# Attention and gated feed-forward on one core: six of seven score tiles transposed by DMA from pair 12, and row sums, v scaling and instruction order rewritten

## The chip, the cores and the metric

The kernel runs on one core of one Trainium2 chip. The metric is the device time of one execution in microseconds (us); lower is better. The core has five engines with a queue each: TensorE (PE; its weight loads are shown apart as PEld), VectorE (DVE), ScalarE (ACT), GpSimd (POOL) and SyncE (SP). Here SP issues every DMA. Each queue runs its instructions strictly in the order in which the program puts them.

## The reference

Eight batches of twelve heads, 448 rows of 64 numbers each. First q and k are normalised by row, then softmax attention, then a feed-forward block with a convolution over three neighbours and a sigmoid gate (q, k, v, the weights and the output are float32; the weights of the second part reach the kernel as float64).

```python
def rmsnorm(x, g):
    rms = np.sqrt(np.mean(x * x, axis=-1, keepdims=True) + 1e-06)
    return x / rms * g
q_n, k_n = (rmsnorm(q, g_q), rmsnorm(k, g_k))
scores = 1.0 / np.sqrt(q.shape[-1]) * np.matmul(q_n, k_n.transpose(0, 1, 3, 2))
attn = np.exp(scores - np.max(scores, axis=-1, keepdims=True))
attn = attn / (np.sum(attn, axis=-1, keepdims=True) + 1e-9)
x = np.matmul(attn, v)                 # then heads side by side: [8, 448, 768]
h = np.maximum(x @ w_in, 0.0)          # [8, 448, 1024]
conv_out = sum(conv_w[k] * hp[:, k:k + S, :] for k in range(3))   # hp: h padded by a row
out = (h * (1 / (1 + np.exp(-conv_out)))) @ w_out                 # [8, 448, 768]
```

## The kernel before

**Pairs.** The 96 heads are worked on two at a time: 48 pairs, n = 0 to 47, six to a batch. A pair's 896 query rows are cut into seven tiles of 128, the slots (`SLOTS`, line 510). One slot's scores are a 128x448 tile.

**Attention of a pair.** `load_k`, `load_q` and `v_load` bring 224 KB each. `square` and `square_sum` (line 349) make the sums of squares, `rsqrt` inverts the root by Newton steps, `apply_rms` scales, `qk_transpose` turns q and k on TensorE, and `qk_hi`/`qk_lo` write each as a high and a low float16 half. `scores` multiplies with three float16 products per slot (high by high, low by high, high by low). `soft_max` (DVE), then `soft_exp` (ACT), which also writes the row sums into `rsum`.

**Two ways to turn a slot.** The product with v needs the exponentials e transposed. In the first way `p_transpose` (line 582) does it on TensorE with four float32 transposes, and `p_evac` (line 589) copies the result from PSUM to `PT`. In the second way `p_hi` and `p_lo` (lines 560, 568) split e into two float16 halves in a buffer `ph`, and `p_turn` (line 575) turns both halves in one DMA transpose from `ph` to `PT`. `nd(n)` (line 516) says how many slots of a pair go the second way: none for n below `n1` = 8, then 4.

**The product with v.** `pv` (line 652) first multiplies the columns that came through TensorE in float32 (eight products of 64 rows; 448 columns each where no slot goes by DMA, 192 with four slots by DMA), and then those that came by DMA as 24 float16 products (256 columns with four slots). For it `v_scaled` (line 631) multiplies v in place by a power of two, `v_hi` (line 637) casts that to float16 and `v_lo` (line 640) subtracts to get the low half.

**The row sums.** `sum_step` (line 596) adds 1e-9 and inverts the 128x7 tile `rsum` on DVE, `sum_transpose` (line 604) turns it on TensorE, `sum_evac` copies it to `rT`, `sum_store` writes it to DRAM (`rd`), and two `sum_load` read it back over all partitions (`rB`). `x_scale` (line 674) multiplies the product by it.

**The feed-forward.** After six pairs a batch's eight `in_part` groups (line 736; 18 products of 448 columns each) run, with relu, convolution, tanh and gate on ACT, DVE and POOL, and then the `out_part` groups (line 798; 24 products of 384 columns each). They are spread between the pairs of the next batches. Until about 140 us the kernel also converts the weights on DVE.

**What sets the order.** Every step has a planned due time (`at`), what it needs (`needs`, line 915), and a cost on each engine that may run it (`options`, line 1167). A planner in the kernel simulates the engines with these, picks one ready step after another, and so fixes both the engine of each step and the order of every queue before the program is made. `PH` (line 20) holds its numbers, `BUFS` (line 104) the count of buffers of each kind: `ph` 3, `PT` 2, `e` 3, and two PSUM buffers `t` for everything that TensorE transposes. `LAT` (line 1297) says how long after a step's end another engine may use it.

```
521:        if ("PT", n) not in rings.setdefault("PT", Ring(BUFS["PT"])).d:
575:    def p_turn(n, j):
577:        nc.sync.dma_start_transpose(
1046:            yield "pv", n - BUFS["PT"], pvs(n - BUFS["PT"])[-1]
1298:        "PE": dict(PE=0.0, DVE=0.2, ACT=0.2, POOL=0.2, SP=0.2, DMA=0.2),
1299:        "DVE": dict(PE=0.06, DVE=0.13, ACT=0.13, POOL=0.16, DMA=0.17),
```

## Time and profile before

| What | Value |
|---|---|
| Median of 3 runs | 979.03 us (978.38 to 981.58) |
| The profiled execution | 978.28 us |
| its span, first to last instruction | 976.5 us |
| PE busy | 893.8 us, 92% |
| DVE busy | 777.3 us, 80% |
| ACT busy | 680.4 us, 70% |
| POOL busy | 660.1 us, 68% |
| DMA: share of the 16 engines' span, hardware queue | 52.1% |

The profile is of one execution. Busy time is the time in which an engine ran at least one instruction. The span is 1.8 us shorter than that execution's own time. A window table gives busy time for stretches of the span and the clock that TensorE was granted, where 1.00 is its upper level, 2.4 GHz, and 0.50 the lower, 1.2 GHz.

### The profile page before, as it was taken

How to read it: one execution, taken by the hardware profiler on the slowest of the kernel's cores; microseconds unless marked ns; L12 is line 12 of the kernel's file. 1: busy time of each engine (PE TensorE's matmuls, PEld its weight loads, DVE VectorE, ACT ScalarE, POOL GpSimd, SP SyncE). 2: the span in 40 equal slices, each digit the busy share in tenths (PEclk: the TensorE clock that was granted, in tenths of full speed). 3: DMA queues.
4: the chain of work that ended last, by engine and by line, in shares of the span. 5: the costliest groups of instructions: out<-in, count | busy, mean ns of one | idle time of the engine just before them, and what ended most of it. 6: DMA issues, size and time to landing. Idle time of an engine off the chain costs nothing.

```text
span 976.5 us, 18886 instructions
## 1 busy us (share of the span) xinstructions
PE 893.8 (92%) x6590; PEld 522.6 (54%) x6590; DVE 777.3 (80%) x1349; ACT 680.4 (70%) x1564; POOL 660.1 (68%) x723
## 2 busy tenths in 40 slices
PE   1777688978999799999999999999999999999988
PEld 0344344545656366655665566556665665556545
DVE  6999979899689967699789977898889966992540
ACT  3678667776666777679688776788788776785331
POOL 2489868886687758498688767587778864772120
PEclk9788669998999999999999999999999999999999
DMA  9945423343773677555765667446684565244001
GB/s 215 247 105 148 126 57 76 64 101 71 155 160 75 107 125 149 116 110 103 153 133 122 125 133 148 102 92 139 144 163 92 109 148 100 51 94 107 17 16 50
DMA packets 259759, 111.02 MB, mean 114 GB/s; under 512 B 220928, under 2 KB 256080, under 8 KB 259664
## 3 DMA queue, kind: packets, MB, share of 16 engines
q1 hardware_dynamic: 259664, 109.82, 52.1%
q8 instruction: 52, 0.85, 0.3%
q14 instruction: 43, 0.35, 0.1%
HBM read 56.65 MB, written 11.18 MB: 69 GB/s over the span
## 4 chain that ended last, share of the span: by engine, by line
PE 49%; DVE 12%; POOL 6%; issue 3%; ACT 3%; DMA 1%; SPq 0%; POOLq 0%; ACTq 0%; DVEq 0%
POOL ph L89 1%; POOL gring L89 1%; POOL sq L89 1%; DMA PT<-ph 1%; DVE st L351 1%; DVE ph L89 1%; POOL x L89 1%; POOL st L386 1%; DVE c_(1_4_3520 L763 0%; POOL st L375 0%; DVE carry L788 0%; PE m_('o'_7_0_0_12066 L812 0%; PE m_('o'_5_3_0_10563 L812 0%; PE m_('o'_3_3_0_7531 L812 0%; PE m_('o'_1_3_0_4495 L812 0%
## 5 line engine op out<-in xcount | busy, mean ns | idle before, releaser
L742 PEld LDWEIGHTS <-wi 128*128 128x128 f16 x1152 | 108.7, 98 | 99.8 <-issue 16.6
L812 PEld LDWEIGHTS <-gring 128*128 128x128 f16 (+1 forms) x1056 | 101.3, 100 | 66.4 <-issue 16.9
L89 POOL TENSOR_TENSOR sq<-qkf,st 112x512 f32<-112x512 f32 x80 | 96.0, 1214 | 2.8 <-ACT wi L254 1.0
L89 POOL TENSOR_TENSOR x<-rB,x 128x448 f16<-128x448 f32 x48 | 57.2, 1191 | 49.3 <-ACT x L77 39.5
L633 POOL TENSOR_SCALAR v<-v,vsc 112x512 f32<-112x512 f32 x42 | 72.0, 1718 | 17.8 <-DVE vsc L186 16.1
L543 PEld LDWEIGHTS <-qT 64*128 64x128 f16 x864 | 32.5, 96 | 71.1 <-issue 55.5
L351 DVE TENSOR_REDUCE st<-sq 112x16 f32<-112x1024 f32 x48 | 58.0, 1209 | 3.2 <-ACT sq L345 2.4
L669 PEld LDWEIGHTS <-vp 112*64 112x64 f16 x960 | 51.1, 110 | 9.7 <-issue 7.8
L441 POOL COPY qz<-qT 64x128 f16<-64x128 f16 x90 | 37.4, 416 | 25.8 <-DVE qT L432 23.1
L89 POOL TENSOR_TENSOR vp<-v,vp 112x512 f16<-112x512 f32 x38 | 46.3, 1219 | 8.9 <-ACT vp L77 6.6
L345 ACT ACTIVATE sq<-qkf 112x1024 f32<-112x1024 f32 x33 | 34.9, 1059 | 4.5 <-DMA qkf<-in_q_dram 4.5
L89 POOL TENSOR_TENSOR sq<-qkf 112x1024 f32<-112x1024 f32 x15 | 30.1, 2005 | 4.5 <-PE t_('qk'_7_0_1418 L412 2.3
L471 DVE TENSOR_REDUCE vacc<-v 112x1 f32<-112x512 f32 x48 | 32.2, 671 | 0.3
L77 ACT CAST vp<-v 112x512 f16<-112x512 f32 x36 | 22.2, 618 | 11.4 <-PE m_('v'_18_4614 L669 3.4
L600 DVE TENSOR_SCALAR rsum<-rsum 128x7 f32<-128x7 f32 x48 | 20.8, 432 | 8.2 <-ACT e_(29_6_7231 L555 1.5
L812 PEld LDWEIGHTS <-carry 128*64 128x64 f16 x192 | 20.2, 114 | 10.8 <-issue 4.1
L375 POOL TENSOR_SCALAR st<-st 112x32 f32<-112x32 f32 (+1 forms) x53 | 19.1, 360 | 10.0 <-DVE st L388 4.2
L386 POOL TENSOR_TENSOR st<-st 112x32 f32<-112x32 f32 (+1 forms) x25 | 10.1, 406 | 22.5 <-DVE st L381 19.4
L812 PEld LDWEIGHTS <-wi 128*128 128x128 f16 (+1 forms) x192 | 19.6, 102 | 9.3 <-ACT wi L77 0.5
L788 DVE COPY carry<-gring 128x128 f16<-128x128 f16 x32 | 19.2, 599 | 5.8 <-POOL gring L89 5.8
L543 PEld LDWEIGHTS <-qz 128*128 128x128 f16 x144 | 14.1, 100 | 16.5 <-issue 6.4
L89 DVE TENSOR_TENSOR sq<-qkf,st 112x512 f32<-112x512 f32 x16 | 22.7, 1424 | 0.0
(3733 smaller groups left out, 3134.2 us busy)
## 6 DMA issues: line engine op xcount, KB each, us to landing
qkf<-in_k_dram SPq DMA_DIRECT2D x48, 224.0 KB
qkf<-in_q_dram SPq DMA_DIRECT2D x48, 224.0 KB
v<-in_v_dram SPq DMA_DIRECT2D x48, 224.0 KB
rB<-rd SPq DMA_DIRECT2D x96, 112.0 KB
wo<-in_moe_w_in_dram SPq DMA_DIRECT2D x12, 512.0 KB
gring<-in_moe_w_out_dram SPq DMA_DIRECT2D x16, 384.0 KB
PT<-ph SPq DMA_TRANSPOSE x160
rd<-rT SPq DMA_DIRECT2D x48, 3.5 KB
```

The lines of the kernel that those rows point to most:

```text
L77: (nc.scalar.copy if e == "ACT" else elementwise(e).tensor_copy)(dst, src)
L89: elementwise(e).tensor_tensor(dst, a, b, op=op)
L345: nc.scalar.activation(sq, old("qkf", n), AF.Square)
L351: nc.vector.tensor_reduce(old("st", m)[:, 0, n - m].rearrange("p i s -> p (i s)"), old("sq", n).rearrange("p i h t d -> p (i h t) d"), axi ...
L441: e.tensor_copy(z[HALF[h], :, HALF[h]], old("qT", n)[HALF[h], :, t0 : t0 + 64])
L471: nc.vector.tensor_reduce(old("vacc", b)[:PB, i : i + 1], old("v", n).rearrange("p h t d -> p (h t d)"), axis=AX.X, op=ALU.max, apply_abso ...
L543: nc.tensor.matmul(ps[u][:, :S], lhs, kt[r, w], start=(i == 0), stop=(i == 2))
L600: nc.vector.tensor_scalar(r, r, 1e-9, None, op0=ALU.add)
L633: elementwise(on["v_scaled", n]).tensor_scalar(v, v, old("vsc", n // NP)[:PB, 1:2], None, op0=ALU.mult)
L669: nc.tensor.matmul(ps[HALF[h], out[h]], v[:, w, h, k], pt[:PB, a, k, col[h]], start=(i == 0 and k == 0), stop=(i == 2 and k == NB - 1),)
L742: nc.tensor.matmul(ps[:, :S], wi[:, wl, c, fc * P : (fc + 1) * P], old("x", b * NP + c)[:, xl], start=(i == 0), stop=(i == 3 * NP - 1),)
L812: nc.tensor.matmul(ps[p0 : p0 + m, :NO2], g, wo[:, wl, fc, half * NO2 : (half + 1) * NO2], start=(i == 0), stop=(i == 3 * NFC - 1),)
```

## The change

- `nd(n)` is now 0 for n below 11 and 6 from n = 11 (the twelfth pair) on: 37 pairs turn six slots by DMA and one on TensorE, where 40 pairs turned four and three. That is 222 DMA transposes for 160.
- In those pairs the float32 part of `pv` has 64 columns and the float16 part 384. For pairs 8, 9 and 10 nothing goes by DMA any more, and `pv` is float32 alone, 448 columns.
- `v_scaled` is gone. Where slots go by DMA, `v_hi` casts and scales v in one instruction, `v_lo` scales and subtracts in one (on DVE alone; it could run on POOL), and `p_evac` scales what it copies. Where none does, `x_scale` multiplies by the scale.
- Row sums: `sum_transpose` follows the exponentials directly, `sum_evac` adds 1e-9 while it copies, and `sum_invert` inverts the turned 7x128 tile on DVE ahead of `sum_store`.
- For n below 15 a new step `square_fold` (POOL) adds the two halves of each row of squares, and `square_sum` (DVE) adds up 32 numbers a row in place of 64.
- `ph` has 4 buffers (3), `x` 11 (12). The planner's numbers differ, a result of DVE, ACT or POOL counts as ready for TensorE half a microsecond later than before (`slack`), DMA transposes no longer wait in the plan for one another to land (`LOOSE`), and `qk_transpose` waits in the plan for the scores two pairs back.

```diff
 PH = dict(
-    T0=18.19, N0=5, T=16.2, ti=26.477, si=4.987, so=6.734, hop=0.568, beta=0.028, wi0=-41.512,
...
-    ct=1.5, p_vs=0.938, p_ph=0.39, p_pl=0.493,
+    T0=15.375, N0=5, T=15.778, ti=25.464, si=4.835, so=9.006, hop=0.535, beta=0.028,
...
+    p_ev=7.57, sp=0.263, nbulk=5, p_rs=0.078, p_sq=1.188, p_w=0.5, v0=4.399, nd=[6, 6], n1=11,
+    nf=15, slack=0.5, sw=0, pvs=2, ct=1.5, p_vs=0.938, p_ph=0.535, p_pl=0.631, dg=2,
...
-        qkf=3, sq=2, st=2, qT=2, kT=2, qz=2, v=8, sst=6, e=3, PT=2, x=12, c=3,
-        rB=2, vacc=2, vsc=4, cwb=3, s=3, t=2, m=3, rd=2, rsum=2, rT=2, mx=10, h=2, ph=3, vp=2,
+        qkf=3, sq=2, st=2, qT=2, kT=2, qz=2, v=8, sst=6, e=3, PT=2, x=11, c=3,
+        rB=2, vacc=2, vsc=4, cwb=3, s=3, t=2, m=3, rd=2, rsum=2, rT=2, mx=10, h=2, ph=4, vp=2,
...
+    def square_fold(n):
+        x = old("sq", n).rearrange("p i h t d -> p (i h t) d")
+        binary("POOL", x[:, :, : D // 2], x[:, :, : D // 2], x[:, :, D // 2 :], ALU.add)
+
     def square_sum(n):
...
-            old("sq", n).rearrange("p i h t d -> p (i h t) d"), axis=AX.X, op=ALU.add,
+            x[:, :, : D // 2] if folded(n) else x, axis=AX.X, op=ALU.add,
...
+        return n < PH["nf"]
...
-        return 0 if n < PH["n1"] else 2 * PH["dg"]
+        return 0 if n < PH["n1"] else PH["nd"][n % 2]
...
+        if nd(n):
+
+            copy_scaled(*args, old("vsc", n // NP)[:PB, 1:2])
         else:
-            nc.vector.reciprocal(r, r)
+            copy(*args)
...
     def sum_evac(n):
-        copy(on["sum_evac", n], new("rT", n, [NS, P], F32), old("t", ("r", n))[:NS, :P])
+        dst, src = new("rT", n, [NS, P], F32), old("t", ("r", n))[:NS, :P]
+        if on["sum_evac", n] == "ACT":
+            nc.scalar.activation(dst, src, AF.Copy, bias=1e-9)
+        else:
+            nc.vector.tensor_scalar(dst, src, 1e-9, None, op0=ALU.add)
+
+    def sum_invert(n):
+        nc.vector.reciprocal(old("rT", n), old("rT", n))
...
-    def v_scaled(n):
-        v = old("v", n).rearrange("p h t d -> p (h t d)")
-        elementwise(on["v_scaled", n]).tensor_scalar(
-            v, v, old("vsc", n // NP)[:PB, 1:2], None, op0=ALU.mult
-        )
...
     def v_hi(n):
-        copy(on["v_hi", n], new("vp", n, [PB, 2, 2, NB, D], F16)[:, 0], old("v", n))
+        copy_scaled(
+            on["v_hi", n], new("vp", n, [PB, 2, 2, NB, D], F16)[:, 0], old("v", n),
+            old("vsc", n // NP)[:PB, 1:2],
+        )
 
     def v_lo(n):
         vp = old("vp", n)
-        binary(on["v_lo", n], vp[:, 1], old("v", n), vp[:, 0], ALU.subtract)
+        nc.vector.scalar_tensor_tensor(
+            vp[:, 1], old("v", n), old("vsc", n // NP)[:PB, 1:2], vp[:, 0],
+            op0=ALU.mult, op1=ALU.subtract,
+        )
...
+        return S if nd(n) == NS else nd(n) // 2 * P
...
-        wd = nd(n) // 2 * P
+        wd = width(n)
...
     def x_scale(n):
-        t = old("rB", n)
-        nc.vector.tensor_tensor(t, old("m", ("v", n))[:, :S], t, op=ALU.mult)
+        t, ps = old("rB", n), old("m", ("v", n))[:, :S]
+        if nd(n):
+            nc.vector.tensor_tensor(t, ps, t, op=ALU.mult)
+        else:
+            nc.vector.scalar_tensor_tensor(
+                t, ps, old("vsc", n // NP)[:, 1:2], t, op0=ALU.mult, op1=ALU.mult
+            )
...
         elif name == "qk_transpose":
             yield "apply_rms", *a
+            yield "scores", n - 2, NG - 1
...
+    for e in ("DVE", "ACT", "POOL"):
+        LAT[e]["PE"] += PH["slack"]
...
+    LOOSE = {("p_turn", "p_turn"), ("p_turn", "p_evac"), ("v_load", "v_load"), ("load", "load")} | {
+        ("load_k", "load_q"), ("load_q", "load_k"), ("sum_load", "sum_load")
+    }
```

The diff's table of numbers doesn't show what the planner now does with the queues. Three places do; rows between are left out at "...".

TensorE, end of pair 24 (`t_('p'_24_j` is slot j's transpose, `t_('r'_24` the row sums', `m_('v'_24` the product with v), before:

```order
L585 MATMUL t_('p'_24_4_5961<-ident,e_(24_4_5944 112x128 x4
...
L585 MATMUL t_('p'_24_5_5978<-ident,e_(24_5_5959 112x128 x4
...
L585 MATMUL t_('p'_24_6_5999<-ident,e_(24_6_5969 112x128 x4
...
L605 MATMUL t_('r'_24_6011<-ident,rsum_5783 7x128
...
L660 MATMUL m_('v'_24_6071<-PT_5830,v_4162 64x192 x8
L669 LDWEIGHTS vp_5891
L669 MATMUL m_('v'_24_6071<-PT_5830,vp_5891 64x256
```

and now:

```order
L595 MATMUL t_('p'_24_6_5830<-ident,e_(24_6_5814 112x128 x4
L612 MATMUL t_('r'_24_5838<-ident,rsum_5605 7x128
...
L680 MATMUL m_('v'_24_5884<-PT_5660,v_4286 64x64 x8
...
L689 LDWEIGHTS vp_5764
L689 MATMUL m_('v'_24_5884<-PT_5660,vp_5764 64x384
```

Two of three transposes are gone, the float32 products are a third as wide and the float16 products half as wide again; between the two parts of the product other work now stands.

VectorE at the same place, before (`sst` is a slot's maximum, `rB` the scaled product, `rsum` the row sums):

```order
L547 TENSOR_REDUCE sst_(24_6_5957<-s_(24_6_5940 128x1
L676 TENSOR_TENSOR rB_5870<-m_('v'_23_5832,rB_5870 128x448
L600 TENSOR_SCALAR rsum_5783<-rsum_5783 128x7
L77 CAST x_5988<-rB_5870 128x448
L602 RECIPROCAL rsum_5783<-rsum_5783 128x7
L89 TENSOR_TENSOR vp_5935<-v_4455,vp_5935 112x512
```

and now (`rT` is the turned row sums, `vp` the halves of v):

```order
L557 TENSOR_REDUCE sst_(25_1_5827<-s_(25_1_5790 128x1
L82 TENSOR_SCALAR vp_5836<-v_4512,vsc_5561 112x512
L480 MEMSET vacc_5845 128x6
L481 TENSOR_REDUCE vacc_5845<-v_5784 112x1
L88 TENSOR_TENSOR ph_76<-e_(25_0_5824,ph_76 128x4x112
L624 RECIPROCAL rT_5857<-rT_5857 7x128
L557 TENSOR_REDUCE sst_(25_2_5874<-s_(25_2_5849 128x1
```

The two small operations ahead of TensorE's row-sum transpose are gone from VectorE, and one stands behind it, ahead of the store.

SP, where pairs 28 and 29 meet (`PT` is written by the transposes, `rd` and `rB` carry the row sums), before:

```order
L577 DMA_TRANSPOSE PT_6827<-ph_78 128x8x128
L613 DMA rd_7077<-rT_7062 7x128
L577 DMA_TRANSPOSE PT_7101<-ph_76 128x8x128
L619 DMA rB_7130<-rd_7077 64x448
L826 DMA out_dram<-c_('o'_3_0_1_7103 128x384
```

and now:

```order
L587 DMA_TRANSPOSE PT_6647<-ph_76 128x8x128
L627 DMA rd_6729<-rT_6691 7x128
L587 DMA_TRANSPOSE PT_6647<-ph_77 128x8x128
L633 DMA rB_6771<-rd_6729 64x448 x2
L587 DMA_TRANSPOSE PT_6647<-ph_78 128x8x128
L587 DMA_TRANSPOSE PT_6647<-ph_79 128x8x128
L627 DMA rd_6857<-rT_6826 7x128
L587 DMA_TRANSPOSE PT_6869<-ph_76 128x8x128
L633 DMA rB_6901<-rd_6857 64x448 x2
```

Four of pair 28's six transposes (`PT_6647`) stand close behind one another on the one queue, with the row sums of pair 27 between them; the store of pair 28's row sums follows, and pair 29's first transpose behind that.

## Rows read from the trace of the kernel before

**Rows 1.** The page's busy times: engine, us, share of the span, instructions.
```profile
PE 893.8 (92%) x6590; PEld 522.6 (54%) x6590; DVE 777.3 (80%) x1349; ACT 680.4 (70%) x1564; POOL 660.1 (68%) x723
```

**Rows 2.** Windows: stretch, length, busy us (instructions) by engine, clock, DMA share, GB/s.
```profile
0.00:48.00 48.00, 20.79 (x87) 10.62 (x89) 37.79 (x84) 22.87 (x51) 17.62 (x42) 0.91 0.95 235
48.00:144.00 96.00, 73.76 (x378) 38.52 (x375) 88.50 (x161) 70.10 (x174) 79.10 (x64) 0.75 0.42 111
144.00:240.00 96.00, 85.19 (x560) 46.02 (x559) 87.54 (x140) 70.70 (x158) 75.81 (x75) 0.94 0.35 74
...
400.00:448.00 48.00, 46.81 (x351) 26.87 (x351) 43.34 (x72) 37.97 (x87) 35.04 (x38) 1.00 0.46 92
...
512.00:560.00 48.00, 47.51 (x408) 28.16 (x404) 45.29 (x68) 38.47 (x88) 39.43 (x45) 1.00 0.64 126
```

**Rows 3.** The same view, the stretch from 240 to 904 us as a whole.
```profile
240.00:904.00 664.00, 648.48 (x5161) 390.95 (x5159) 537.91 (x936) 497.25 (x1149) 478.23 (x535) 1.00 0.58 120
```

**Rows 4.** The page's chain that ended last: shares of the span by engine.
```profile
PE 49%; DVE 12%; POOL 6%; issue 3%; ACT 3%; DMA 1%; SPq 0%; POOLq 0%; ACTq 0%; DVEq 0%
```

**Rows 5.** Waits of all engines: engine, line, for whom; us in total, times, longest.
```profile
PE t_('qk'_0_1_166 L412 <- POOL sq L89: 18.9, 1, 18.9
```

**Rows 6.** PE's timeline from 491 to 499 us: start, length, what, count.
```profile
491.23 0.60 PE L585 MATMUL t_('p'_24_6_5999<-ident,e_(24_6_5969 128*112 128x128 f32 x4
491.66 0.81 PE L812 MATMUL m_('o'_2_2_1_5927<-wo,gring 128*128 128x384 f16 x4
...
496.11 1.52 PE L660 MATMUL m_('v'_24_6071<-PT,v 112*64 112x192 f32 x16
497.46 1.48 PE L669 MATMUL m_('v'_24_6071<-PT,vp 112*64 112x256 f16 x24
498.87 0.36 PE L543 MATMUL s_(25_4_6121<-kT,qT 64*128 64x448 f16 x1
```

**Rows 7.** PE's timeline from 161 to 165.5 us, a pair with no slot by DMA.
```profile
161.83 3.23 PE L660 MATMUL m_('v'_6_1595<-PT,v 112*64 112x448 f32 x16
164.99 0.60 PE L412 MATMUL t_('qk'_8_0_1622<-ident,sq 112*128 112x112 f32 x4
```

**Rows 8.** Groups by shape, PEld: busy us, mean ns of one, idle before, releasers.
```profile
L669 PEld LDWEIGHTS <-vp 112*64 112x64 f16 x960 | 51.1, 110 | 9.7 <-issue 7.8
...
L660 PEld LDWEIGHTS m_('v'_25_6305<-PT,v 112*64 112x64 f32 x16 | 1.1, 136 | 0.5 <-DVE c_(3_1_6277 L763 0.4
```

**Rows 9.** Groups by shape, DVE and POOL.
```profile
L633 POOL TENSOR_SCALAR v<-v,vsc 112x512 f32<-112x512 f32 x42 | 72.0, 1718 | 17.8 <-DVE vsc L186 16.1 <-DVE st L388 1.0
L351 DVE TENSOR_REDUCE st<-sq 112x16 f32<-112x1024 f32 x48 | 58.0, 1209 | 3.2 <-ACT sq L345 2.4 <-POOL sq L89 0.7
...
L89 POOL TENSOR_TENSOR vp<-v,vp 112x512 f16<-112x512 f32 x38 | 46.3, 1219 | 8.9 <-ACT vp L77 6.6 <-PE t_('qk'_13_0_2804 L412 0.7 <-PE t_('p'_46_5_11508 L585 0.5
...
L471 DVE TENSOR_REDUCE vacc<-v 112x1 f32<-112x512 f32 x48 | 32.2, 671 | 0.3
...
L600 DVE TENSOR_SCALAR rsum<-rsum 128x7 f32<-128x7 f32 x48 | 20.8, 432 | 8.2 <-ACT e_(29_6_7231 L555 1.5 <-ACT e_(41_6_10267 L555 1.3 <-ACT e_(47_6_11712 L555 1.2
...
L602 DVE RECIPROCAL rsum<-rsum 128x7 f32<-128x7 f32 x48 | 9.2, 192 | 0.3
...
L287 DVE SCALAR_TENSOR_TENSOR wo<-wo,wsc 128x768 f16<-128x768 f32 x6 | 6.3, 1057 | 0.9 <-ACT wo L279 0.9
...
L89 DVE TENSOR_TENSOR vp<-v,vp 112x512 f16<-112x512 f32 x2 | 4.8, 2413 | 0.0
```

**Rows 10.** SP's timeline: an issue of a transpose with nothing behind it.
```profile
859.25 1.23 SPq L577 DMA_TRANSPOSE PT<-ph  x1
```

**Rows 11.** Window around that transpose's packets: length, clock, DMA share, GB/s.
```profile
860.00:862.50 2.50, 1.00 0.59 112
```

**Rows 12.** Chain in order of time, two places where a transpose's landing is waited for.
```profile
430.08 4.85 DMA PT<-ph
...
641.85 2.41 DMA PT<-ph
```

More of the change, by code (lines that the diff above doesn't have):

```diff
@@ L1157, in needs @@
             yield "out_evac", *a
+    turns = [(n, j) for n in range(NPAIR) for j in range(nd(n))]
     def back(n, g, i, m=NS):
@@ L1249, in takes @@
             return "t"
-        if name in ("in_part", "out_part") and not a[-2] or name == "pv" and not a[-1]:
+        if name in ("in_part", "out_part") and not a[-2] or name == "pv" and a[-1] == pvs(a[0])[0]:
             return "m"
```

107 lines of the change are left out of this document (58 added, 49 removed).

## The prediction

> **What bounds the kernel now.** I read the page's busy times first. TensorE is busy 92% of the span, and VectorE, next, 80% [rows 1]: the question is what TensorE has to do and when it waits. The windows say when. From 240 to 904 us TensorE is busy 648.5 of 664 us at a granted clock of 1.00 [rows 3]: it idles 15.5 us, and the time of that stretch is TensorE's work. The first 240 us look different: TensorE is busy 20.8 + 73.8 + 85.2 = 179.7 us, with a granted clock of 0.75 from 48 to 144 us, while VectorE is busy 213.8 us there [rows 2]. Of TensorE's 60.3 idle us 18.9 lie ahead of its first instruction [rows 5]; the other 41.4 are waits for the engines that feed it.
>
> The chain that ended last tells the same with one warning: TensorE has 49% of the span, the other named shares come to 25% [rows 4]. So of what the chain names, 66% is TensorE's and a third is not: in stretches such as 400 to 448 and 512 to 560 us, where a batch's convolutions run, VectorE is busy 43.3 and 45.3 of 48 us [rows 2].
>
> All sums below are made against the profiled execution, 978.3 us; the median of the runs is 0.7 us above it.
>
> **1. Six slots for four, pairs 11 to 47: less work on TensorE.** The row-tile transpose of a slot takes TensorE from 491.23 to 491.66, 0.43 us [rows 6]; two fewer are 0.86 us a pair. The product with v took 1.35 us in float32 (192 columns, 496.11 to 497.46) and 1.41 us in float16 (256 columns, to 498.87), together 2.76 us [rows 6]. With 384 columns the float16 part becomes 1.41 x 384/256 = 2.11 us. The float32 part with 64 columns isn't in the trace. With 448 columns it took 3.16 us, from 161.83 to 164.99 [rows 7]; 448 and 192 columns lie on a line through zero (7.07 ns a column), which gives 0.45 us for 64. But its sixteen weight loads kept the load path busy for 1.1 us [rows 8]; if they don't shrink, 1.1 us is the floor. I take 0.8, the middle: no row has loads of 64 columns closer than the float16 part's 24 in 1.41 us, 59 ns apart [rows 6], and sixteen of those would be 0.94. The product then costs 2.91 us, 0.15 more, and a pair saves 0.71 us: 37 pairs, **-26.3 us**. The ends are 0.45 (-39.0 us) and 1.1 (-15.0 us).
>
> The rows say that a load of 64 columns lasts 110 ns in float16 and 136 ns in float32 [rows 8], two at a time. The Trainium skill, page "TensorE: Matmul & The Clock Gate", section "LDWEIGHTS (loading the stationary operand)", says instead that a load takes its columns divided by 1.2 in ns, 53 ns for 64. By that page, as an estimate, the sixteen loads would take 0.85 us, the term would be -24.4 us, and the whole about 950 us.
>
> **2. Pairs 8, 9 and 10 go back to TensorE.** Four more slot transposes are 1.72 us, and the product 3.16 instead of 2.76: 2.12 us a pair, **+6.4 us**.
>
> **3. Waits in TensorE's order, 240 to 904 us.** What waits there are 15.5 us in all. The row sums no longer pass two VectorE operations (0.43 and 0.19 us [rows 9]) before TensorE may turn them, transposes wait less for PSUM since fewer use it, and the planner keeps half a microsecond between a feeder's end and TensorE's use. The gain lies between nothing and 15.5; I take a third, **-5 us**, because the other changes add waits of their own.
>
> **4. The first 240 us.** Fifteen sums of squares add 512 numbers a row in place of 1024: from 1.21 us to about the 0.67 us of the reduction over 512 [rows 9], 8.1 us off an engine that is 92% busy from 48 to 144 us [rows 2]. Some of it will be idle time, so **-5 us**; the ends are nothing and, if TensorE's waits there halve, -20.7 (a rival below).
>
> **What I cost at nothing, and its cover.** *Scaling v.* The 42 scalings (1.72 us each) and 38 subtractions (1.22 us) leave POOL, 118 us [rows 9]; 70 more `p_lo` there at the same 1.22 are 85 us and 15 folds at some 1.2 us are 18, so POOL has less to do. Casts move to ScalarE for copies that leave it, about one for one. *VectorE* loses 48 x 0.62 = 30 us of row-sum steps and the 8.1 us, and gains 48 inversions of a 7x128 tile (between 0.19 and 0.43 us [rows 9]; at 0.25, 12 us) and 37 `v_lo`. One of these costs 0.70 us by the fused instruction on 768 columns (1057 ns x 512/768) and 2.41 by the two subtractions that VectorE ran itself [rows 9]; at 1.0 they are 37 us. The balance is +11 us, and VectorE is busy 538 of 664 us [rows 3]. That cover is thin where convolutions run. *The inversion* now stands between the evacuation and the store on SP, and all that SP has behind that store waits with it; what it replaces stood in the same path, two steps for one.
>
> *DMA.* One transpose keeps the sixteen DMA engines busy for 2.5 x 0.59 = 1.48 us [rows 11], issued at 859.25 [rows 10], its packets over by 862.5. SP is held 1.23 us for each [rows 10], so 62 more are 77 us of SP and 92 us of DMA. In the stretch from 240 to 904 us the share is 0.58 [rows 3]; some 70 more transposes in a stretch about 26 us shorter make (385 + 104) / 638 = 0.77. That is room on average, and I charge nothing; where transfers bunch, a transpose lands late, and then the product with v is late next.
>
> **The sum:** -26.3 + 6.4 - 5 - 5 = -29.9 us; 978.3 - 29.9 = **948.4 us**, forecast 948.
>
> **Rivals.** *A. The other third of the chain holds.* Term 1 is worth something only where TensorE ends the wait. If the third of the chain that is VectorE's and POOL's [rows 4] doesn't shorten, it gives 26.3 x 0.66 = 17.4 us, and term 3 nothing: 978.3 - 17.4 + 6.4 - 5 = 962 us. For it: VectorE at 90 to 94% where convolutions run, with `v_lo` added. Against it: TensorE is busy 97 to 99% in those same windows [rows 2].
>
> *B. The beginning gains more.* If half of TensorE's 41.4 us of waits in the first 240 us go, term 4 is -20.7 and the time 933 us. For it: a clock of 0.75 there, which a TensorE with fewer waits might be granted at 1.00; against it: VectorE, which is nearly full, loses only 8 us.
>
> *C. Slower: the sixth transpose is late.* All six go through one queue and one set of DMA engines, and the float16 product of a pair, 24 instructions of TensorE's fixed order, waits for the last of them; everything behind it on TensorE waits too. The trace has a landing that took 4.85 us on the chain where another took 2.41 [rows 12], so a transpose can lose a transpose's time or more to others. If each of 37 products waits one transpose's 1.48 us, that is +54.8 us: 1003 us. It decides from 29.9 / 37 = 0.81 us of waiting a pair on. Against it: a share of 0.77, a fourth `ph` buffer, and other work placed between the two parts of the product. The Trainium skill, page "VectorE: DVE Perf Modes", section "Rules for kernel authors", speaks for it: it has a 128x128 transpose go to TensorE if PSUM will do as its target, and to DMA otherwise; the trace agrees as far as a single one goes, 0.43 us on TensorE against 1.48 us of DMA [rows 6, 11].
>
> **How the numbers follow.** The forecast has 0.55, with 935 to 961 as its own range from the ends of term 1; A has 0.20, B 0.10, C 0.10, and 0.05 is left for gains and waits that cancel within 0.3%, which is about what a measurement of this kernel can tell from no change. Faster: 0.55 + 0.20 + 0.10 = 0.85; same 0.05; slower 0.10. The range reaches from a little under B (928) to a little over A (968) and leaves out C and the case of no change.
>
> **What would show it.** Right: TensorE's busy time falls by about 20 us to 874; a pair's float32 product takes about 0.8 us and its float16 product 2.1; TensorE stays 97% busy or more from 240 us to the end of the pairs; the DMA share there is near 0.77, and a transpose is seldom named as what TensorE waits for. A would show as TensorE idle in the windows of the convolutions with VectorE at 95% or more; B as a granted clock nearer 1.00 before 150 us; C as waits of TensorE's float16 products for DMA of a microsecond a pair. A float32 product of 1.1 us or more would take term 1 to its small end.

## The result, and the profile of the changed kernel

The changed kernel takes **971.12 us** (median of 3 runs, 969.74 to 971.19) against 979.03 (978.38 to 981.58): ratio 0.9911, 95% interval 0.9887 to 0.9935. It is faster, by 8 us where 31 were forecast, and outside the range of 928 to 968. Later runs of the kernel before scatter from 970.8 to 983.2 us, with medians of 977.8 to 979.4, so the gain is one of medians. The profiled execution has a span of 969.1 us against 976.5.

The page's busy times after the change; [rows 1] has those of before:

```profile
PE 862.1 (89%) x6270; PEld 468.1 (48%) x6270; DVE 816.0 (84%) x1329; ACT 689.4 (71%) x1572; POOL 642.2 (66%) x688
```

TensorE lost 31.7 us of work, more than the forecast's 20. VectorE gained 38.7 us; the forecast had 11. The windows answer to [rows 2, 3], with the same columns (stretch, length, busy us and instructions of PE, PEld, DVE, ACT, POOL, clock, DMA share, GB/s); the last, in a convolution stretch, is new:

```profile
48.00:144.00 96.00, 69.32 (x365) 33.82 (x362) 83.89 (x152) 69.24 (x173) 61.57 (x52) 0.82 0.46 117
144.00:240.00 96.00, 90.49 (x583) 48.83 (x580) 89.81 (x159) 73.11 (x166) 65.14 (x62) 1.00 0.20 50
240.00:904.00 664.00, 623.60 (x4848) 342.43 (x4847) 580.17 (x913) 503.05 (x1144) 479.76 (x517) 0.97 0.76 149
400.00:448.00 48.00, 45.06 (x349) 24.32 (x346) 46.60 (x66) 34.71 (x77) 31.93 (x34) 1.00 0.64 125
512.00:560.00 48.00, 40.48 (x316) 20.74 (x316) 45.67 (x62) 37.00 (x84) 45.14 (x44) 0.86 0.62 123
...
528.00:544.00 16.00, 9.83 (x62) 4.66 (x59) 16.00 (x18) 10.39 (x23) 15.86 (x14) 0.75 0.68 139
```

From 240 to 904 us TensorE now idles 40.4 us where it idled 15.5. About half of the 25 us more lies in two convolution stretches: from 528 to 544 us it idles 6.2 us (0.4 before), from 736 to 768 us 7.7 us (0.4). VectorE is full there, 16.00 of 16 us from 528 to 544, and the granted clock is 0.75, so the work that is left costs more as well. The DMA share, 0.76, is the forecast 0.77. The chain that ended last, shares of the span by engine, answers to [rows 4]:

```profile
DVE 38%; PE 30%; ACT 8%; issue 8%; POOL 7%; DMA 6%; SPq 1%; ACTq 0%; POOLq 0%; DVEq 0%
```

TensorE fell from 49% to 30% and VectorE rose from 12% to 38%. The engine that the sum was made on no longer has the largest share of the chain.

*Where the time came from and went.* On TensorE's timeline the last product with v of pair 10 ends at 238.9 us (before: 250.2), that of pair 47 at 895.3 (903.9). By pair 10 the new kernel leads by 11.4 us, at the end of the pairs by 8.5. The forecast had +1.4 us up to there (terms 2 and 4) and -31.3 from there on (terms 1 and 3); measured are -11.4 and +2.8. The lead is partly borrowed: by the end of pair 10 the new order has issued 48 of the output products where the old one had issued 73, and 245 score products for 252, some 5 us of work put off (24 output products take 3.9 us where nothing waits), of which some 4 fall into the 37 pairs. So about 6 us are won in the first 240 us, and the 37 pairs on which six slots go by DMA gave next to nothing.

What won and what lost shows on TensorE. The first 240 us, before and after:

```profile
0.00:240.00 240.00, 179.74 (x1021) 95.15 (x1022) 213.82 (x383) 163.67 (x381) 172.53 (x179) 0.86 0.50 121
0.00:240.00 240.00, 180.08 (x1055) 93.07 (x1056) 211.35 (x386) 167.84 (x396) 154.15 (x164) 0.93 0.47 112
```

TensorE idles as long as before (60.3 and 59.9 us); what rose is the granted clock, from 0.86 to 0.93. In the pairs behind that it went the other way. Three times the clock fell to its lower level, in the middle of a convolution stretch:

```profile
321.00:331.20 10.20, 5.48 (x24) 2.01 (x23) 10.20 (x14) 8.29 (x19) 5.71 (x6) 0.50 0.52 100
536.00:549.70 13.70, 8.49 (x35) 3.06 (x36) 13.67 (x16) 8.71 (x22) 12.77 (x14) 0.50 0.67 121
751.10:764.70 13.60, 8.85 (x40) 3.72 (x42) 13.54 (x17) 8.30 (x20) 12.59 (x15) 0.50 0.59 118
```

TensorE worked 22.8 us there, where before it worked 3.3 us at 0.50 in all these pairs. An output product of 384 columns lasts 0.53 us in these stretches and 0.33 us at 1.00 (medians), so the lower clock cost the 37 pairs some 7 us more than before, as an estimate from these durations, or 10 if the work there went at half the pace.

The term itself is there. PE's timeline (start, length, what, count) of a pair with six slots, for [rows 6]:

```profile
483.92 0.69 PE L680 MATMUL m_('v'_24_5884<-PT,v 112*64 112x64 f32 x16
484.53 1.31 PE L765 MATMUL m_('i'_3_0_5840<-x,wi 128*128 128x448 f16 x6
...
486.45 2.14 PE L689 MATMUL m_('v'_24_5884<-PT,vp 112*64 112x384 f16 x24
488.52 0.74 PE L765 MATMUL m_('i'_3_0_5840<-x,wi 128*128 128x448 f16 x3
```

The float32 product with 64 columns takes 0.61 us (483.92 to 484.53; 0.8 was taken) and the float16 one 2.07 (2.11). A pair saves 0.86 + 2.76 - 2.68 = 0.94 us, and 37 pairs 34.8, between the term's ends.

VectorE's groups by shape (busy us, mean ns of one, idle before), for the operations of [rows 9] that changed:

```profile
L624 DVE RECIPROCAL rT<-rT 7x128 f32<-7x128 f32 x48 | 44.9, 934 | 7.5 <-ACT rT L619 7.3
L659 DVE SCALAR_TENSOR_TENSOR vp<-v,vsc,vp 112x512 f16<-112x512 f32 x37 | 41.3, 1116 | 0.2
...
L355 DVE TENSOR_REDUCE st<-sq 112x16 f32<-112x512 f32 x15 | 10.2, 678 | 3.4 <-POOL sq L88 3.3
```

The inversion takes 0.934 us, not 0.25. Turned, the tile has 7 rows of 128 numbers in place of 128 rows of 7, and by these two shapes the duration goes by the numbers in a row: (934 - 192) / (128 - 7) = 6.1 ns each. The 128x7 pair of operations had cost 30.0 us in all [rows 9]; the new one costs 44.9.

A mean hides what the second half of the loss is. Two answers of the trace for single lines give the duration of one as minimum, median and maximum in ns. In the kernel after:

```profile
L659 DVE SCALAR_TENSOR_TENSOR vp<-v,vsc,vp x37: 728/752/2517, 226.4 to 871.6; 112x512 f16<-112x512 f32 x37
...
L624 DVE RECIPROCAL rT<-rT x48: 929/933/941, 43.0 to 888.1; 7x128 f32<-7x128 f32 x48
```

and in the kernel before:

```profile
L600 DVE TENSOR_SCALAR rsum<-rsum x48: 148/171/2228, 43.7 to 894.2; 128x7 f32<-128x7 f32 x48
```

An addition to seven numbers takes 0.17 us in the middle case and up to 2.2 us; the inversion of a 7x128 tile never varies. What the long ones have in common is GpSimd beside them: of the 128 convolution steps of line 786, the 32 with GpSimd idle took 0.67 us on average, the 49 with GpSimd busy throughout 1.18. The reductions of score tiles, which read PSUM alone, take 0.61 us either way. Counted so over all VectorE operations, such lengthening is some 150 us of VectorE's time before and some 170 us after. How much of its growth (40.6 us as a sum over instructions) that is depends on the count: with each kernel's own means it is some 145 and 169 us, 24 us of waiting; with one common duration per operation for both kernels it is 154 and 166, 12 us. The rest, 17 to 29 us, is work: the inversion and `v_lo` added more than that, but the planner took other steps off VectorE (`apply_rms` from 22.8 us to 5.2). The Trainium skill, page "SBUF — State Buffer", section "Who interferes with whom", says that VectorE and GpSimd share a pair of ports, that a VectorE instruction with two inputs in SBUF contends with a GpSimd one that reads SBUF, and that one with a single input outside the two-port modes does not. The rows agree in that convolution step and `v_lo` with two inputs vary, inversion and reduction don't. The addition varies with its one input, so by that rule it would run in a two-port mode, which no run here shows.

How this reaches TensorE can be followed in one place, the timeline of all engines of the changed kernel around 542 us:

```profile
539.78 1.89 POOL L88 TENSOR_TENSOR sq<-qkf 112x1024 f32<-112x1024 f32 x1
...
540.50 3.62 DVE L796 SCALAR_TENSOR_TENSOR c_(3_7_6570<-c_(3_7_6570,hbuf 128x448 f32<-128x448 f32 x1
...
541.63 1.03 POOL L88 TENSOR_TENSOR ph<-e_(28_0_6595,ph 128x448 f16<-128x448 f32 x1
...
542.62 1.03 POOL L88 TENSOR_TENSOR wi<-c_(3_6_6477,wi 128x448 f16<-128x448 f32 x1
...
543.61 1.41 POOL L88 TENSOR_TENSOR ph<-e_(28_1_6615,ph 128x448 f16<-128x448 f32 x1
...
544.16 0.57 ACT L76 CAST wo<-c_(3_7_6570 128x448 f16<-128x448 f32 x1 [4.18 <-DVE c_(3_7_6570 L796]
...
544.78 0.53 PE L835 MATMUL m_('o'_3_0_0_6533<-wo 128*64 128x384 f16 x1 [2.09 <-ACT wo L76]
```

The gate's multiplication, 0.61 us where GpSimd is idle, is held for 3.62 us beside four GpSimd instructions in a row, two of them `p_lo` (`ph`), of which GpSimd now has 203 in place of 133. That it is held by them is read from the times, not tested alone. ScalarE's cast waits 4.18 us for it, and TensorE's output product 2.09 us for the cast. A hold of 3.62 us comes twice in the change, at 540 and at 754 us, in the two stretches where TensorE's idle time grew most; before, the longest of the 64 such multiplications took 2.2 us.

### The profile page after: what moved, and what is told of

The parts are those of the page before. It is cut to its first block, busy times and chain, and to the rows that moved or that the text cites. A ratio compares the mean times of both kernels' runs of the same rounds, so it can differ in the third digit from the quotient of the medians.

```text
span 969.1 us, 18435 instructions
## 1 busy us (share of the span) xinstructions
PE 862.1 (89%) x6270; PEld 468.1 (48%) x6270; DVE 816.0 (84%) x1329; ACT 689.4 (71%) x1572; POOL 642.2 (66%) x688
## 4 chain that ended last, share of the span: by engine, by line
DVE 38%; PE 30%; ACT 8%; issue 8%; POOL 7%; DMA 6%; SPq 1%; ACTq 0%; POOLq 0%; DVEq 0%
DMA rB<-rd 2%; POOL ph L88 2%; DVE rT L624 2%; DVE vp L659 2%; DVE st L355 2%; DVE carry L811 1%; POOL sq L88 1%; DVE kT L438 1%; DVE st L381 1%; POOL gring L88 1%; ACT ph L76 1%; DMA qkf<-in_q_dram 1%; DVE wo L203 1%; DVE qT L440 1%; DVE rB L697 1%
## 5 line engine op out<-in xcount | busy, mean ns | idle before, releaser
L88 POOL TENSOR_TENSOR sq<-qkf,st 112x512 f32<-112x512 f32 x91 | 119.4, 1330 | 8.9 <-DVE st L381 6.0
L355 DVE TENSOR_REDUCE st<-sq 112x16 f32<-112x1024 f32 (+1 forms) x48 | 49.8, 1043 | 8.2 <-ACT sq L344 4.7
L624 DVE RECIPROCAL rT<-rT 7x128 f32<-7x128 f32 x48 | 44.9, 934 | 7.5 <-ACT rT L619 7.3
L449 POOL COPY qz<-qT 64x128 f16<-64x128 f16 x81 | 29.9, 369 | 21.5 <-DVE qT L440 13.2
L659 DVE SCALAR_TENSOR_TENSOR vp<-v,vsc,vp 112x512 f16<-112x512 f32 x37 | 41.3, 1116 | 0.2
L88 POOL TENSOR_TENSOR sq<-sq 112x512 f32<-112x512 f32 x15 | 20.8, 1383 | 18.6 <-ACT sq L344 18.2
L76 ACT CAST x<-rB 128x448 f16<-128x448 f32 x32 | 17.9, 560 | 20.6 <-DVE rB L697 16.9
L381 DVE SCALAR_TENSOR_TENSOR st<-st 112x32 f32<-112x32 f32 (+1 forms) x46 | 24.6, 535 | 2.8 <-POOL st L384 1.3
L80 ACT ACTIVATE vp<-v,vsc 112x512 f16<-112x512 f32 x30 | 21.5, 716 | 1.0 <-DVE vsc L185 0.9
L283 POOL TENSOR_SCALAR wi<-wi,wsc 128x1024 f32<-128x1024 f32 x5 | 15.9, 3180 | 6.4 <-ACT wi L278 3.6
```

The costliest lines, as they stand in the source:

```text
L88: elementwise(e).tensor_tensor(dst, a, b, op=op)
L355: nc.vector.tensor_reduce(old("st", m)[:, 0, n - m].rearrange("p i s -> p (i s)"), x[:, :, : D // 2] if folded(n) else x, axis=AX.X, op=AL ...
L381: v.scalar_tensor_tensor(dst, x, c, z, op0=ALU.add, op1=ALU.mult)
L449: e.tensor_copy(z[HALF[h], :, HALF[h]], old("qT", n)[HALF[h], :, t0 : t0 + 64])
L624: nc.vector.reciprocal(old("rT", n), old("rT", n))
L659: nc.vector.scalar_tensor_tensor(vp[:, 1], old("v", n), old("vsc", n // NP)[:PB, 1:2], vp[:, 0], op0=ALU.mult, op1=ALU.subtract,)
```

## The experiments

Three theories at first. **V**: VectorE's added time is what the gain went to. **D**: the transposes by DMA are late. **S**: the store of the row sums, behind the inversion on SP, holds the other DMAs. After twelve runs a fourth, **L**: VectorE's time passes on at about 0.4 us per us whatever TensorE has to do. VectorE, DMA and so on below stand for busy time in the profile. "In the frozen order" means that every queue is as in the kernel that was edited; otherwise the planner laid out the order anew.

**One inversion more, in the frozen order of the change.**

```diff
+    spare = const.tile([7, P], F32, name="spare")
         nc.vector.reciprocal(old("rT", n), old("rT", n))
+        nc.vector.reciprocal(spare, old("rT", n))
```

> The changed kernel, with a second inversion of each 7x128 tile into a spare tile right behind the first: 48 x 0.93 = 45 us more on VectorE, nothing else, and the store of the row sums waits for the first alone. Theory V: 20 to 45 us slower, 991 to 1016. Rivals D and S: within 5 us of 971.

Measured 990.40 us, 19 more than the change, for 45 us that nothing waits for (VectorE busy 850.7). That is 0.6 us under the range of V and far from those of D and S: VectorE's time is not covered in full.

**The low half of v left out, in the frozen order** (the product reads the high half in its place). "Run 1" below is the narrow inversion in the frozen order, further down.

```diff
     def v_lo(n):
-        vp = old("vp", n)
-        nc.vector.scalar_tensor_tensor(
-            vp[:, 1], old("v", n), old("vsc", n // NP)[:PB, 1:2], vp[:, 0],
-            op0=ALU.mult, op1=ALU.subtract,
-        )
+        pass
...
-        (a, w), v, pt = PV3[i], old("vp", n), places(n)[1]
+        (a, _), w, v, pt = PV3[i], 0, old("vp", n), places(n)[1]
```

> The changed kernel without the low half of v: VectorE's 37 fused instructions (1.12 us each, 41 us) are left out, and the products that used the low half read the high half instead, so that TensorE does the same work. Theory V: 12 to 28 us faster, 943 to 959, much as in run 1, though the row sums' way is as in the changed kernel. Rivals D and S: within 3 us of 971.

Measured 960.31 us: 10.8 less for 41 us removed, 0.26 us per us. V again, at a smaller rate, 1 us above its range; D and S had no change.

**One of a pair's six transposes issued twice, in the frozen order.**

```diff
+        for _ in range(2 if j == 1 else 1):
             nc.sync.dma_start_transpose(
```

> The changed kernel, with one of the six DMA transposes of each of the 37 pairs issued twice: 37 x 1.48 = 55 us more of all DMA engines and 37 x 1.23 = 46 us more of SP. Rival D: the late landings grow, 15 to 55 us slower, 986 to 1026. Theory V: within 5 us of 971, since DMA has room at a share of 0.76.

Measured 1012.97 us, 42 more for 55 us of DMA and 46 us of SP. Its waits of all engines (us in total, times, longest) name what is late:

```profile
DVE rB L698 <- DMA rB<-rd: 50.1, 23, 7.2
```

The row sums' loads stand behind the transposes on SP, and VectorE waits for them: 8.8 us in the change, 50.1 here. So D has something for it as well, and V's guess that the DMA engines had room for 55 us more was wrong: not much more would fit.

**Half a transpose, in the frozen order** (only the high half is turned and read).

```diff
...
-            old("ph", (n, j)).rearrange("q a k p -> q (a k p)"),
+            old("ph", (n, j))[:, 0].rearrange("q k p -> q (k p)"),
...
```

> Beside the change, in its very order of instructions, each transpose by DMA turns only the high half of a slot, and the products that want the low half read the high one; the low half is still formed. It leaves out the low halves' term of the product. 222 transposes move half the bytes: 222 x 0.74 = 164 us of the sixteen DMA engines fall away, nothing else does. Theory V (VectorE's added time is what the gain was lost to, the DMA engines have slack): 971, at best 968. Theory D (the transposes' time decides): the run with one of six transposes doubled passed on 42 us for 55 us of DMA, so halving all gives back 10 us or more, 945 to 961. In between: both engines are near their limit, 962 to 967.

Measured 967.77 us. The DMA share from 240 to 904 us fell from 0.76 to 0.49 and TensorE's busy time there is what it was:

```profile
240.00:904.00 664.00, 623.36 (x4846) 341.80 (x4845) 581.35 (x911) 501.40 (x1139) 476.95 (x514) 0.97 0.49 104
```

Taking away some 164 us of transfers gave 3.4 us. D falls as the cause, as far as the DMA engines go: they had little room left, but were not what was lost to. SP's time is not tested by it: an issue still takes SP 1.21 us (1.26 in the change), and VectorE's waits for the row sums' loads, 0.4 us before and 11.9 us in all in the change, are still there.

**The inversion as 128x7 ahead of TensorE's transpose, in the frozen order** (the addition of 1e-9 left out). "Run 4" below is the run without the low half of v.

```diff
     def sum_transpose(n):
+        nc.vector.reciprocal(old("rsum", n), old("rsum", n))
         nc.tensor.transpose(
...
-        nc.vector.reciprocal(old("rT", n), old("rT", n))
+        pass
```

> The changed kernel with every queue's plan kept, but the row sums inverted as the 128x7 tile ahead of TensorE's transpose (0.19 us, as in the kernel before) in place of the 7x128 tile behind it (0.93 us); the added 1e-9 is left out, which float32 cannot hold beside sums of 1 and more. That takes 48 x 0.74 = 36 us off VectorE. Theory V (VectorE's time is the bound where convolutions run): TensorE's idle time from 240 us on falls from 40 towards 25 us and the time by 10 to 25 us, to 946 to 961. Rival D (late DMA transposes hold TensorE): within 3 us of 971. Rival S (the store of the row sums on SP, behind the inversion, holds the other DMAs): a gain too, but then run 4 shows none.

Measured 991.02 us, outside of every expectation: 26 us less of VectorE, and 20 us slower. PE's waits (for whom, us in total, times, longest) show why; three of 36 at this transpose, 41 us in all, where the change has two with 4.2:

```profile
PE t_('r'_20_4893 L613 <- DVE carry L812: 3.3, 1, 3.3
...
PE t_('r'_44_10732 L613 <- DVE carry L812: 2.7, 1, 2.7
...
PE t_('r'_4_1155 L613 <- DVE rsum L612: 2.5, 1, 2.5
```

The order of the change puts the transpose of the sums early; with a VectorE step in front of it TensorE stands in line for VectorE's queue. **The same edit with the order laid out anew**:

> The change with the inversion as one 128x7 operation (0.19 us in place of 0.93) ahead of TensorE's transpose of the row sums, as in the kernel before, and the planner told so, so that the order is laid out anew; the addition of 1e-9 is left out. VectorE loses 48 x 0.74 = 36 us. The same edit in the frozen order made TensorE wait for the sums and came to 991. Theory V: with the order laid out anew the waits of TensorE go and 36 us x 0.3 to 0.4 arrive, 957 to 962. Rival (the place decides: TensorE, in order, waits at the transpose for an operation that stands late in VectorE's queue): 975 to 990. Theory D: 968 to 972.

Measured 967.54 us (963.95 to 971.21), not to be told from the change, and between the ranges of V and D. VectorE was 804.5 us, only 11.5 less, since the planner gave it other work.

**How much an order is worth.** First the planner is told what the trace shows of the two new operations; then one of its spacings is changed a little.

```diff
-            sum_invert=lambda: [dve(0.25)],
+            sum_invert=lambda: [dve(0.93)],
...
-            v_lo=lambda: [dve(0.69)],
+            v_lo=lambda: [dve(1.1)],
```

> The same work; the planner that sets the order is told the duration that the trace shows for the inversion (0.93 us in place of 0.25) and for the low half of v (1.1 in place of 0.69), so VectorE's queue is laid out for its real load. Theory V with a wrong plan (the loss comes from instructions that are placed as if VectorE were 39 us freer than it is): 958 to 966. Theory V without (VectorE's work itself is too much, no order helps): 968 to 975. Theory D: no change, 971.

> The change's own work in another order: one of the planner's spacings (of the weight stage) 4.835 made 4.9, nothing else. How much the order alone is worth: if orders of the same work lie within 0.3%, 968 to 974, every difference above stands for its edit; if they scatter as the run with the true costs (979) says, 965 to 985, and the edits with a new order are to be read with that much doubt.

Measured 979.20 us with the true durations, and 974.50 with `si` 4.835 made 4.9: the same work in three orders takes 971, 974.5 and 979, the last outside of every expectation. Differences under 8 us between kernels whose order was laid out anew prove nothing, and truer costs did not make a better order.

**Four slots by DMA with the rest of the change** (`nd=[4, 4]`, `n1=8`).

> From pair 8 four of seven slots by DMA as in the kernel before, with the new handling of the row sums and of v kept. TensorE has again its old work from pair 11 on (+32 us beside the change), the DMA engines lose about 72 transposes x 1.48 = 107 us. Theory V: VectorE's load stays about as in the change, and TensorE's work comes back: slower than the change, 985 to 1000. Theory D (the rest of the change costs nothing, the sixth slot is what loses): as before or better by the gain of the first 240 us, 968 to 979.

Measured 1003.71 us, with TensorE at 900.6 and VectorE at 811.3: 32.6 us slower than six slots, for 38.5 us more of TensorE. D falls again, and TensorE's work does count. It is also 24.7 us slower than the kernel before, with as many slots by DMA: the rest of the change lost about three quarters of what six slots gained, as far as planner numbers chosen for six slots are fair to four. **v as in the kernel before, and six slots alone:**

```diff
+    def v_scaled(n):
+        v = old("v", n).rearrange("p h t d -> p (h t d)")
+        elementwise(on["v_scaled", n]).tensor_scalar(
+            v, v, old("vsc", n // NP)[:PB, 1:2], None, op0=ALU.mult
+        )
...
+        binary(on["v_lo", n], vp[:, 1], old("v", n), vp[:, 0], ALU.subtract)
...
-            v_lo=lambda: [dve(0.69)],
+            v_scaled=lambda: [pool(1.5), dve(0.4)],
+            v_lo=lambda: [pool(1.16), dve(0.62)],
```

The second has the narrow inversion as well.

> The change with v handled as in the kernel before (scaled in place on GpSimd, 1.72 us each, its low half by GpSimd or VectorE; no scale in the evictions of the probabilities), six slots by DMA and the row sums as in the change; the order is laid out anew. VectorE loses up to 41 us, GpSimd gains 72 to 115 us. Theory V (VectorE's time is the loss): leaving the low half of v out altogether gave 11 us; with GpSimd doing it 958 to 966. Rival (GpSimd, 642 us of 969 busy in the change, has no more room): 971 to 985.

> Only the sixth and fifth slot: v as before, the row sums inverted as 128x7 ahead of TensorE's transpose (the addition of 1e-9 left out), and the new planner, order laid out anew. VectorE loses 77 us beside the change. The forecast's main term alone (TensorE's work falls by 32 us and nothing takes its place): 945 to 952. Theory V with 0.3 to 0.4 us passed on per us of VectorE: 971 - 23 to 31 = 940 to 952 too. If the new handling of sums and of v is not what the gain was lost to (DMA, or the order): 965 to 985.

Measured 977.47 and 975.03 us: both miss V and lie in the ranges of its rivals, that GpSimd has no more room, and that the new handling of the sums and of v is not what the gain was lost to. That does not refute V, since its premise did not come about either. VectorE did not fall by 77 us in the second; the page's busy times are

```profile
PE 860.7 (88%) x6270; PEld 470.7 (48%) x6270; DVE 825.2 (85%) x1349; ACT 677.1 (70%) x1561; POOL 711.1 (73%) x723
```

While GpSimd took over v, the planner gave VectorE other steps, `apply_rms` (18 of them, 5 in the change) and `p_lo` (35, 19), and VectorE waited more beside a busier GpSimd: a convolution step (line 786 in the change) took 0.95 us on average before, 1.04 in the change, 1.13 here. **Both VectorE additions off** (narrow inversion, no low half of v):

> The change with the inversion as 128x7 ahead of the transpose (the addition of 1e-9 left out) and the low half of v left out (the product reads the high half in its place); the order is laid out anew. VectorE loses 36 + 41 us beside the change, no other engine gains work. Theory V: the two reliefs add, 971 - 4 - 11 = 956 or less; if relief counts more the more there is of it, 945 to 952. Rival (the DMA engines or GpSimd are the next limit behind VectorE): no better than with the low half left out alone, 958 to 962.

Measured 955.05 us with VectorE at 765.5, in V's range; the rival's begins 3 us above it, less than orders scatter. Though VectorE now has less than the 777.3 us of before, TensorE still idles 37.3 us from 240 to 904 us:

```profile
240.00:904.00 664.00, 626.73 (x4883) 345.81 (x4882) 545.31 (x884) 494.61 (x1135) 465.87 (x523) 0.97 0.75 146
```

**Was VectorE covered in the kernel before?** One inversion of a constant 7x128 tile more for each pair, in that kernel's own order.

```diff
+    spare = const.tile([7, P], F32, name="spare")
+    nc.vector.memset(spare, 1.0)
...
             nc.vector.reciprocal(r, r)
+            nc.vector.reciprocal(spare, spare)
```

> The kernel before, in its own order, with one more inversion of a 7x128 tile (a constant, nothing waits for it) behind each pair's inversion of the row sums: 48 x 0.93 = 45 us of VectorE and nothing else. The forecast took VectorE's time for covered as long as TensorE has its 894 us of work: then 979 to 983. Theory L (VectorE's time passes on at about 0.4 us per us whatever TensorE has to do, as it does beside the change): 979 + 18 = 997, 993 to 1001.

Measured 998.20 us, ratio 1.019 (1.017 to 1.021), 19 us for these 43:

```profile
L605 DVE RECIPROCAL spare<-spare 7x128 f32<-7x128 f32 x48 | 42.7, 890 | 0.0
```

and the window of 240 to 904 us, beside [rows 3]:

```profile
240.00:904.00 664.00, 638.13 (x5026) 381.83 (x5024) 566.91 (x969) 492.19 (x1135) 481.00 (x533) 0.99 0.59 118
```

TensorE, "97 to 99% busy", hid little more than half of it; of the 19 us, 15.7 lie between the ends of pairs 10 and 47. L came as expected, and the full cover of the forecast did not exist.

**Work moved off VectorE.** To the change with the narrow inversion, which leaves out the addition of 1e-9: the carried rows copied by ScalarE; the square-root steps but one on GpSimd; both. Then the second edit alone on the change and on the kernel before.

```diff
-            rsqrt=lambda: [dve(0.23)] if a[1] == 1 else [dve(0.23), pool(0.6 if a[1] in (4, 7, 8) else 0.3)],
+            rsqrt=lambda: [dve(0.23)] if a[1] == 1 else [pool(0.6 if a[1] in (4, 7, 8) else 0.3)],
...
-        nc.vector.tensor_copy(carry[:, b // 2 % 2, :, fc], old("g", (b, fc))[:, :, S - 64 :])
+        nc.scalar.copy(carry[:, b // 2 % 2, :, fc], old("g", (b, fc))[:, :, S - 64 :])
...
-            in_carry=lambda: [dve(0.32)],
+            in_carry=lambda: [act(0.3)],
```

> The change with the narrow inversion ahead of TensorE's transpose (967.5) and the 32 copies of the carried rows (0.60 us each on VectorE, 19 us) on ScalarE; order laid out anew. Theory L: 967.5 - 0.4 x 19 = 960, 956 to 964. Rival (ScalarE has no room, or orders scatter more than that): 966 to 975.

> The change with the narrow inversion ahead of TensorE's transpose (967.5) and all steps of the reciprocal square root but one on GpSimd: some 46 us leave VectorE, some 38 us come to GpSimd; order laid out anew. Theory L: 967.5 - 0.4 x 46 = 949, 944 to 955. Rival (GpSimd's work slows VectorE's: an instruction of 0.19 us alone takes 0.5 to 1.6 us beside GpSimd, and GpSimd's own queue gets longer): 963 to 975.

> Both of the moves above together (carried rows to ScalarE, square-root steps to GpSimd): VectorE loses some 65 us beside the change with the narrow inversion (967.5). Theory L: 967.5 - 26 = 942, 936 to 950. Rival (ScalarE or GpSimd take over as the limit): 955 to 975.

> The change itself with one edit: all steps of the reciprocal square root but one on GpSimd (some 42 us leave VectorE), order laid out anew. Theory L: 971 - 0.4 x 42 = 954, 949 to 960. If the best run so far (950) owed its gain to the narrow inversion and the edit together, or to a lucky order: 962 to 972.

> The kernel before with the same edit (some 30 us leave VectorE, some 25 come to GpSimd), order laid out anew. Theory L: 979 - 0.4 x 30 = 967, 962 to 972, since VectorE's time passes on there too. The forecast's view (TensorE's work ends that kernel, VectorE is covered): 976 to 982.

| Kernel | Measured us | VectorE busy us |
|---|---|---|
| narrow inversion, carried rows on ScalarE | 968.19 (966.35 to 972.71) | 790.8 |
| narrow inversion, square-root steps on GpSimd | 950.06 (948.26 to 950.96) | 768.4 |
| both moves | 958.52 (953.76 to 959.36) | 771.7 |
| the change, square-root steps on GpSimd | 974.13 (970.92 to 979.05) | 800.3 |
| before, square-root steps on GpSimd | 987.00 (983.80 to 990.03) | 758.1 |

One hit of L and four misses; two of the four lie in their rivals' ranges, the last two in neither. The second is the best kernel of this study: ratio to before 0.9699 (0.9677 to 0.9722), 21 us under the change. Its window shows TensorE idle 33.2 us where the change has 40.4:

```profile
240.00:904.00 664.00, 630.75 (x4893) 345.94 (x4893) 550.19 (x873) 502.97 (x1144) 486.87 (x605) 0.98 0.76 146
```

But on the change itself the same edit gave nothing, and on the kernel before it lost 9 us (ratio 1.0104, 1.0068 to 1.0141) though VectorE had 19 us less: with 0.4 us per us expected, orders scatter by more than the edit is worth. So the 950 probably owes something to a lucky order, which no run separates, and L is no law for kernels whose order is laid out anew.

**All runs together.** Fourteen kernels have six slots by DMA and no wait of their own (the change, and all runs above but the doubled transposes, the narrow inversion in the frozen order, four slots, and the two on the kernel before). A straight line through VectorE's busy time (765.5 to 850.7 us) and the measured time (950 to 990) rises 0.375 us per us, with a scatter of 4.2 us; where VectorE has the 777.3 us of before, the line is at 958.7 us. Busy time includes the waiting beside GpSimd, so the line is a correlation and no proof. In frozen orders the rate was 0.26 (low half of v out), 0.43 (second inversion) and 0.44 (kernel before) per us of instructions; per us of VectorE's busy time, as in the line, it was 0.33, 0.56 and 0.61.

TensorE's idle time from 240 to 904 us, set out by slots and by VectorE's busy time (us), tells that VectorE's growth is not all:

| Slots by DMA | VectorE 758 to 777 | VectorE 809 to 816 |
|---|---|---|
| four | 15.5 (before), 19.5 (before, square-root steps on GpSimd) | 25.9 (before, one inversion more), 28.7 (four slots with the rest) |
| six | 37.3 (both off), 33.2 (the 950 us kernel) | 40.4 (the change) |

VectorE's growth adds 6 to 13 us of idle time with four slots and 3 to 7 with six; two more slots add 12 to 22, as far as different orders may be compared.

## Why the prediction was wrong

**The step that failed** is "What I cost at nothing, and its cover": VectorE's balance, which was taken as +11 us and hidden because TensorE is 97 to 99% busy.

- *The size.* +38.7 us of busy time, not +11. The inversion "between 0.19 and 0.43 us" was 0.934, outside its own bounds: they came from tiles of 7 numbers a row, where 128 were to be inverted. That alone is 48 x (0.934 - 0.25) = 33 us. The Trainium skill, page "VectorE: DVE Perf Modes", section "First, the fixed hardware budget", has the reciprocal divide iteratively with a repeat count of eight. It gives no duration; the trace has 6.1 ns for each number, where a reduction of 448 numbers takes 0.61 us, 1.4 ns for each. `v_lo` at 1.0 us was right in size (1.116 on average), but 0.752 in the middle case; the rest goes with waiting beside GpSimd, which the sum had nowhere else. The rows of before held the hint: 0.43 us for an addition to seven numbers and 0.19 for their inversion [rows 9], where the first is a mean of 0.17 and of waits up to 2.2.
- *The cover.* Busy 97 to 99% told that TensorE rarely waits, not that it would not wait more. 43 us on VectorE cost the kernel before 19 us. The gate followed above sits in a chain from VectorE over ScalarE to TensorE, and TensorE, in order, put nothing into that wait.
- *What stands behind term 1*, "the time of that stretch is TensorE's work". It held for the work of before; with some 35 us less of it, TensorE idles 33 to 37 us even where VectorE is as busy as before, so a saved microsecond no longer arrives in full.
- *Term 3* had the wrong sign: -5 us forecast; TensorE's idle time from 240 to 904 us rose by 24.9.

**How the 23 us part** (971.1 against 948.4). On TensorE, in pairs 11 to 47: term 1 saved 34.8 us, idle time took back 25.0, the lower clock some 7 to 10, and work put off from the beginning some 4. That makes 1 to 4 us more than before, and 2.8 were measured where -31.3 were forecast. The first 240 us hide 13 of these 34 us, by a way that was not forecast. By cause, as an estimate by the line above, 12 to 15 us of the 23 are VectorE's growth (to 958.7 us from the 971.1 measured, or from the 973.2 of the line). The table of idle times gives VectorE a smaller share. The other 8 to 10 are gone even with VectorE as before: TensorE's work does not pass on one for one either. That is **rival A**, at 962 us, which had 0.20: its mechanism, other engines ending the wait in the convolution stretches, is what the windows show, though not for its reason alone. What makes TensorE wait with VectorE as before is not settled. The halved transposes leave at most 3.4 us to the DMA engines; VectorE's waits for the row sums' loads behind the transposes on SP are a candidate that no run tests alone.

**What was right.** *Term 1* in size, at the upper clock: 34.8 us where 26.3 stood, within its ends, with 0.61 us for the float32 product in place of 0.8. With four slots in the change's surroundings 32.6 us were lost, so it does pay where VectorE is the same. *Term 4* was right in one size alone: the reductions over 512 take 678 ns, as taken. Its way, fewer waits, did not come, since TensorE idles 59.9 us in the first 240 where it idled 60.3. The lead of 11.4 us at pair 10 is a clock that rose from 0.86 to 0.93 and some 5 us of work put off, with *term 2* (6.4 us) to pay out of it; why the clock rose no run shows, and for the forecast it is luck. So with **rival B**: a sign of it came, 0.82 for 0.75 from 48 to 144 us, but not its half of the waits. *DMA*: 0.76 for 0.77. **Rival C** did not come: TensorE's products waited for a transpose twice, 0.8 us in all. Its point of decision is near, though, since one transpose more of six cost 42 us. Three slips in the working moved nothing: the ends of term 1 give 936 to 960 us and not 935 to 961, 62 x 1.23 is 76, and VectorE and POOL have 18 of the 74 points of the chain that were named, a quarter and not the third that rival A gives them.

## What to carry to other kernels

An engine that is busy 98% does not fully cover one that is busy 80%: if the second feeds the first in order, its time passes on in part, here 0.26 to 0.44 us per us of instructions put in or taken out. Nor does a saving on the busier engine arrive in full: its waits, and here its clock, take some of it back. The cheapest look is a useless operation that nothing waits for, in the frozen order, before the change is made. Price an operation by the numbers in a row and by its median with its neighbours idle, and look at minimum and maximum: a mean far above the median is a wait, and whatever moves to the engine next door may buy more of it. Where a planner lays out the order, measure a few orders of the same work before a difference of 1% is believed.

## What was not expected of the hardware

- A VectorE instruction of 0.61 us took 3.62 us, past the ends of three GpSimd instructions in a row. The Trainium skill, page "SBUF — State Buffer", section "Who interferes with whom", says of the two-port modes that whoever issues first has the shared ports for the whole instruction; the rows don't show who held them, only that the wait outlasted three of GpSimd's.
- Inverting 7x128 numbers takes 0.934 us and 128x7 numbers 0.192 us, five times less for the same 896.
- Sixteen float32 products of 64 columns take 0.61 us, 38 ns each, though a load of weights for such a product lasts 136 ns [rows 8].
- Halving 222 transposes by DMA gave 3.4 us, and doubling 37 of them cost 42.
